# Another hand-planned order for an attention + MLP block on one core, and a later place for the last MLP's weight loads

## The chip, the core and the metric

The kernel runs on one core of a Trainium2 chip. The metric is the device time of one execution in microseconds. The core has five instruction streams that run side by side: TensorE (PE, matmuls; its weight loads are listed as PEld), VectorE (DVE), ScalarE (ACT), GpSimd (POOL), and SyncE (SP), which here issues nearly all DMAs. Each stream runs in its program order and waits on semaphores for the others.

## The reference

A transformer block with modulation, for 2048 tokens of width 640. `A_x`, all weights and `c` are bfloat16.

```python
mod = (_silu(c) @ w_mod).reshape(c.shape[0], 6, 1, -1)
sa, ca, ga, sb, cb, gb = (mod[:, 0], mod[:, 1], mod[:, 2], mod[:, 3], mod[:, 4], mod[:, 5])
h = _layernorm(x) * (1 + ca) + sa
x = x + ga * _A_ref(h, A_wqkv, A_wo)                              # 32 heads of 20, full softmax attention
h = _layernorm(x) * (1 + cb) + sb
x = x + gb * _B_ref(h, B_w_gate, B_w_up, B_w_down)                # ((h @ w_gate) * (h @ w_up)) @ w_down, width 1536
```

## The kernel before

The program is made in two steps. First a planner, written in Python in the kernel's own file, simulates the five engines with a duration for every piece of work (class `Sched`, and `pick_pe` for PE) and so fixes in which order each engine's instructions stand. Then `emit_program` writes each engine's list with the semaphore waits that the dependences need. The chip follows the order; when an instruction really starts is decided by the semaphores. The planner's numbers, such as a due time or a gate, act on the chip only through the order that results.

**The work.** The queries are cut into seven chunks (512, then six of 256). For each chunk there are eight groups of four heads; chunk times group is an *item*, 57 in all, since the last one is cut in two halves of 128 queries. Items run one after another. Within an item, the scores of a head against 128 keys at a time are computed on PE (matmul `QT`, `KT`, L1546) into PSUM banks. Most scores go to ACT, which takes two banks at a time and writes the exponentials to `PP` (L1583, 812 instructions, numbered by *progress*: progress g means that g of them have been issued in the plan). The remaining scores, in groups of four banks, are done without ACT: DVE makes an integer `DB` (L1607) and two further DVE steps and one product on POOL or DVE make the two terms `DSS` (L1639, L1647, L1659 on POOL or L1644 on DVE). Exponentials and terms are multiplied with V on PE (L2220). At the end of an item, DVE transposes the sums (`OT`, L1739), the division follows (L1747), DVE transposes back (`OcT`, L1756), and SP's copies place the rows in `Ocp` (L1768).

**What PE does beside it.** Between score matmuls PE gets three kinds of other work: probability times V (called P), projections and MLP matmuls in steps (called X: Q, K and V projections, the output projection `wo`, `Ocp`, the transposes of `h2T`, gate and up from `stg` or `stx`, down from `wd`; L982 and L978), and padding matmuls on an identity (L2553, L2581). The MLP of a chunk runs while the next chunk's attention runs; the MLP of the last chunk (`h2Tc`, `hprodc`, `xckc`) has nothing beside it and closes the kernel.

**What decides the order.** `pick_pe` is asked whenever PE is free in the plan. A score batch that is ready goes first. Otherwise named constants decide. Those that the change touches, times in nanoseconds:

- `HOLD`: PE is left idle if the next score is ready within this time.
- `FILL_MIN`: if PE's activity in the last 3413 ns of the plan is below it, X work goes ahead of P work. Before that test stands one with a fixed `FILL_HARD` of 3600, under which padding is placed.
- `PVMIN`, `PVMAX`, `PVCAP`, `PVTOL`, `PV_KEEP`: how many units of P work are needed before a batch of it starts (directly behind a score, and otherwise), the most that one takes, how far it may run past the next score, and how many free banks must remain before the next item's P work opens a bank.
- `X_LATE`, `X_HALF`: when an X step that would end after the next score is ready is split in two halves.
- `EAGER`, `D_LATE`, `D_RES`: how early DVE's scores ride along with a score batch, when they get a batch of their own, and when X work leaves banks for them.
- `XBACK`, `LKTOL`: when DVE takes the product of DVE's path from POOL, and how long POOL may hold the port that it shares with DVE when DVE has work for it.
- `STEAL_GAP`: how long ACT must be free to take an evacuation from DVE; allowed only before `STEAL_END` (66.2 us of the plan) and behind the last exponential.
- `DL`: when DVE's share of an item is due. The change leaves it as it is.

`STAGE` overrides them item by item. When the plan's P work enters an item, the constants go back to the file's defaults and the item's own entries are laid over them:

```python
    def stage(it):
        globals().update(base)
        globals().update(STAGE.get(it, {}))
```

**The last MLP's weights.** Gate and up are loaded in 12 chunks of 128 columns each, 160 KB a load. Chunks 0 to 4 go to buffers that are free once the chunk before the last no longer needs its queries; chunks 5 to 9 to buffers in the region of the projections; 10 and 11 to the ordinary staging buffers `stg`. Each load gets a gate, the progress at which the planner may first place it in SP's list:

```python
gate=int(gstart[NC] - 40) if tail and not use_x else int(gstart[NC - 1]) + 1 + STX_G * fc if tail and fc < nsq else
     NG - STX_T + int(STX_S * (fc - nsq)) if tail else ...
```

`NG` is 812 and `nsq` is 5. Among SP's ready DMAs the planner takes the one with the lowest priority number: output writes have 1, `Ocp` copies of the last two groups of heads 1.05, other `Ocp` copies 2, these weights 22. Once they stand in the list, nothing is overtaken any more: SP waits for each in its turn.

Of the kernel before, what the change touches and what calls it, by code (L numbers as in the profile page):

```python
# [35 lines left out]
STEAL_GAP = 200  # L36
HAM_W = 3413.3
HAM_MIN = 3100.0
LKTOL = 300.0
# [320 lines left out]
def emit_program(nc, sched, nsem_dma=56):  # L360
# [130 lines left out]
PV_KEEP = 2  # L491
# [10 lines left out]
EAGER = 7  # L502
# [3 lines left out]
XBACK = 0  # L506
HOLD = 110
PVTOL = 249
XDPRIO = 1.343
TPRIO = 0.75  # L510
# [20 lines left out]
D_LATE = 16  # L531
D_RES = 20
PVMIN, PVMAX, PVCAP = 2, 7, 12
# [14 lines left out]
FILL_MIN = 4190.746  # L548
# [22 lines left out]
NTERM = 2  # L571

STAGE = {
    0: {"PVMAX": 14, "XDPRIO": 1.343, "D_LATE": 16, "PVTOL": 249, "STEAL_GAP": 200, "EAGER": 4, "PVCAP": 12, "XBACK": 0, "PV_KEEP": 2, "PVMIN": 2, "HOLD": 95, "TPRIO": 0.75, "LKTOL": 300.0, "FILL_MIN": 4190.746, "X_LATE": -179.96, "D_RES": 74},
    1: {"X_HALF": 105.6, "D_RES": 62, "LKTOL": 153.5},
    2: {"DL": 0.376},
    4: {"D_RES": 31, "HOLD": 130.9, "EAGER": 12},
    5: {"D_LATE": 7, "PVMAX": 3},
    6: {"X_LATE": 168.4, "FILL_MIN": 5225.9},
    7: {"DL": 0.501, "EAGER": 12, "X_HALF": 6.3, "PVCAP": 13, "HOLD": 135.2},  # L580
    8: {"PV_KEEP": 2, "X_HALF": 103.9, "LKTOL": 307.3, "HOLD": 78.3},
    10: {"LKTOL": 95.0},
    11: {"DL": 0.443, "X_LATE": 70.4, "STEAL_GAP": 234.3},
    12: {"DL": 0.459, "PVMIN": 2, "D_LATE": 10, "LKTOL": 67.4},
    13: {"DL": 0.417, "HOLD": 108.3, "X_LATE": 6.6, "D_LATE": 17, "PVMAX": 9},
    14: {"HOLD": 73.1, "PVMIN": 2, "STEAL_GAP": 219.5},
    15: {"PVTOL": 269.4, "X_LATE": -109.7},
    18: {"HOLD": 92.2, "D_RES": 79, "PVMAX": 4, "X_HALF": 82.3},
    19: {"DL": 0.471},
    20: {"DL": 0.391, "D_RES": 12, "XBACK": 3, "FILL_MIN": 3591.0, "HOLD": 163.1},  # L590
    21: {"PVCAP": 9, "PVMAX": 2, "D_LATE": 13},
    22: {"HOLD": 191.0},
    23: {"X_HALF": -10.6, "EAGER": 3},
    24: {"DL": 0.464},
    25: {"DL": 0.549, "HOLD": 78.3, "PVMIN": 2},
    26: {"DL": 0.411, "XBACK": 3, "X_LATE": -173.2, "X_HALF": 76.9},
    27: {"DL": 0.473},
    28: {"X_LATE": -150.3, "PVMAX": 2},
    29: {"PVTOL": 317.6, "PVMAX": 4},
    30: {"D_RES": 35, "X_HALF": -38.3},  # L600
    31: {"PVMIN": 2, "FILL_MIN": 4430.1},
    32: {"PV_KEEP": 3, "PVMIN": 2},
    33: {"DL": 0.442, "FILL_MIN": 4061.0, "PV_KEEP": 2, "PVMAX": 10},
    35: {"PVMIN": 7, "LKTOL": 244.1},
    36: {"DL": 0.524, "PVMAX": 2},
    37: {"HOLD": 29.2, "PVTOL": 368.4, "PV_KEEP": 2},
    38: {"X_LATE": -201.5},
    39: {"X_LATE": 136.2},
    41: {"X_HALF": -34.1},
    43: {"XBACK": 0, "HOLD": 184.9},  # L610
    46: {"X_HALF": 35.9},
    48: {"D_LATE": 16, "FILL_MIN": 4750.6},
    50: {"FILL_MIN": 3890.7, "X_HALF": 28.4},
    51: {"X_LATE": -35.5, "XBACK": 0},
    55: {"FILL_MIN": 4927.0, "PV_KEEP": 1},
    56: {"HOLD": 80.1},
}
XHALF = 1
STG_G0, STG_G, XC_G = 12, -10, -20
X_LATE = -24.052  # L620
X_HALF = 0.0
# [2037 lines left out]
```

## Time and profile before

| what | value |
|---|---|
| median of 3 runs | 806.1 us (805.99 to 806.1) |
| the profiled execution | 807.02 us, span 805.2 us |
| PE busy | 789.9 us, 98% |
| ACT busy | 766.0 us, 95% |
| DVE busy | 701.3 us, 87% |
| POOL busy | 375.0 us, 47% |
| first exponential starts, last one starts | 16.3 us, 776.4 us |
| DMA | 64.69 MB, mean 80 GB/s |

The span is the time from the first to the last instruction of the profiled execution; the execution's own time is 1.8 us longer, and the median of the runs is 0.9 us below it. In the lists that follow, a line such as "L1583 ACT" is the instruction written by line 1583 of the kernel, on ACT; "x812" is the count. Times are in microseconds unless marked ns. Matmuls are pipelined and their ends are modelled, so 98% busy is not PE at its peak.

### The profile page before, as it was taken

The page shows a single profiled execution, that of the slowest core. Times are in us where ns is not written, and L with a number is a line of the kernel's source. Part 1 is how long each engine was busy: PE and PEld are TensorE (multiplying, and loading weights), DVE is VectorE, ACT ScalarE, POOL GpSimd, SP SyncE. Part 2 cuts the span into 40 slices and gives each one's busy share as a digit, 9 for nine tenths or more (in the row PEclk, how much of TensorE's full clock was granted, in tenths as well). Part 3 has the DMA queues.
Part 4 walks back from the last instruction along what each step waited for, and adds up shares of the span by engine and source line. Part 5 has one row for each costly group of instructions (what it writes and reads, how often), then busy time and mean ns, then how long its engine had stood idle before and what let it go on. Part 6 is the DMA issues. An engine that isn't in the chain of part 4 may idle for free.

```text
span 805.2 us, 38415 instructions
## 1 busy us (share of the span) xinstructions
PE 789.9 (98%) x16929; PEld 377.9 (47%) x16929; DVE 701.3 (87%) x1392; ACT 766.0 (95%) x853; POOL 375.0 (47%) x388
## 2 busy tenths in 40 slices
PE   8999999999999999999999999999999999999998
PEld 4443423332244443444555555555544554555567
DVE  7887988898989999998899978998789999998654
ACT  6889999999999999999999999999999999999961
POOL 3334455546445554446545464455566433344400
PEclk9999999999999999999999999999999999999999
DMA  9644222202342622110032314311530134414530
GB/s 300 204 130 116 56 56 64 62 24 73 91 108 62 188 64 61 33 40 22 23 89 67 78 54 91 69 48 48 121 73 14 48 81 103 105 33 104 127 64 18
DMA packets 154316, 64.69 MB, mean 80 GB/s; under 512 B 116951, under 2 KB 154151, under 8 KB 154151
## 3 DMA queue, kind: packets, MB, share of 16 engines
q1 hardware_dynamic: 153223, 61.10, 29.8%
q8 instruction: 134, 2.20, 1.1%
q10 hardware_dynamic: 928, 1.15, 0.5%
q14 instruction: 31, 0.25, 0.1%
HBM read 50.63 MB, written 8.99 MB: 74 GB/s over the span
## 4 chain that ended last, share of the span: by engine, by line
PE 52%; ACT 30%; DVE 12%; issue 4%; DMA 2%; SPq 1%; ACTq 0%; POOL 0%; DVEq 0%
ACT PP L1583 30%; PE ps_all L1546 18%; PE ps_all L982 15%; PE ps_all L2220 13%; PE ps_all L978 3%; DVE DB L1607 3%; PE ps_all L1249 2%; DVE hT L1154 1%; DVE st L1084 1%; DMA wm<-in_w_mod_dram 1%; DVE DSS L1644 1%; DVE DSS L1647 1%; DVE DSS L1639 1%; DMA stg<-in_B_w_up_dram 0%; SPq L1310 0%
## 5 line engine op out<-in xcount | busy, mean ns | idle before, releaser
L1583 ACT ACTIVATE PP<-ps_all 128x1024 bf16<-128x1024 f32 x812 | 748.8, 1111 | 5.2 <-PE ps_all L1546 4.5
L1659 POOL TENSOR_TENSOR DSS<-DB,DSS 128x512 bf16<-128x512 bf16 x260 | 295.8, 1158 | 302.6 <-DVE DSS L1647 247.8
L1607 DVE TENSOR_SCALAR DB<-ps_all 128x512 int16<-128x512 f32 x424 | 282.7, 681 | 49.5 <-PE ps_all L1546 47.3
L1546 PE MATMUL ps_all<-QT,KT 32*128 32x256 bf16 (+2 forms) x3648 | 320.0, 286 | 5.5 <-ACT PP L1583 3.3
L1546 PEld LDWEIGHTS ps_all<-QT,KT 32*128 32x128 bf16 x3648 | 93.2, 92 | 206.8 <-ACT PP L1583 153.8
L2220 PE MATMUL ps_all<-PP,Vf 128*32 128x256 bf16 (+2 forms) x2900 | 162.4, 290 | 0.2
L982 PE MATMUL ps_all<-h2T,stg 128*32 128x256 bf16 (+2 forms) x2720 | 124.6, 281 | 0.4 <-DVE DB L1607 0.4
L2220 PEld LDWEIGHTS ps_all<-PP,Vf 128*32 128x32 bf16 (+1 forms) x2900 | 56.3, 94 | 75.7 <-issue 69.6
L2220 PE MATMUL ps_all<-DSS,Vf 128*32 128x256 bf16 (+1 forms) x1496 | 87.4, 290 | 0.4 <-DVE DSS L1644 0.2
L1639 DVE TENSOR_SCALAR DSS<-DB 128x2048 int16<-128x2048 int16 x106 | 74.7, 705 | 0.3
L982 PEld LDWEIGHTS ps_all<-h2T,stg 128*32 128x32 bf16 x2720 | 61.5, 96 | 28.4 <-issue 22.6
L1647 DVE TENSOR_SCALAR DSS<-DB 128x2048 int16<-128x2048 int16 x106 | 72.9, 687 | 0.7 <-PE ps_all L2220 0.7
L982 PE MATMUL ps_all<-wd,hprod 128*32 128x320 bf16 (+1 forms) x1376 | 63.3, 280 | 0.4 <-DVE h2T L1922 0.2
L1644 DVE TENSOR_TENSOR DSS<-DB,DSS 128x2048 bf16<-128x2048 bf16 x41 | 51.3, 1252 | 0.0
L1747 POOL TENSOR_TENSOR OTn<-OT,invT 128x256 bf16<-128x256 f32 (+1 forms) x49 | 36.0, 735 | 32.6 <-DVE invT L1745 32.4
L2220 PEld LDWEIGHTS ps_all<-DSS,Vf 128*32 128x32 bf16 x1496 | 35.3, 95 | 21.9 <-issue 10.7
L982 PEld LDWEIGHTS ps_all<-wd,hprod 128*32 128x32 bf16 x1376 | 30.4, 96 | 18.9 <-issue 13.5
L982 PE MATMUL ps_all<-wV,hT 128*32 128x160 bf16 x1280 | 37.9, 234 | 0.9 <-DVE gab L1457 0.8
L1739 DVE STREAM_TRANSPOSE OT<-ps_all 128x256 f32<-128x256 f32 (+2 forms) x57 | 27.1, 475 | 9.2 <-PE ps_all L2220 8.7
L982 PE MATMUL ps_all<-wo,Ocp 128*32 128x320 bf16 (+1 forms) x648 | 31.1, 283 | 0.7 <-issue 0.3
L1249 PE MATMUL ps_all<-hT,wk 128*32 128x512 bf16 (+1 forms) x360 | 31.5, 382 | 0.1
L982 PEld LDWEIGHTS ps_all<-wV,hT 128*32 128x32 bf16 x1280 | 24.6, 96 | 14.7 <-issue 6.8
(133 smaller groups left out, 561.5 us busy)
## 6 DMA issues: line engine op xcount, KB each, us to landing
stg<-in_B_w_gate_dram SPq DMA_DIRECT2D x74, 160.0 KB
stg<-in_B_w_up_dram SPq DMA_DIRECT2D x74, 160.0 KB
KT<-k_rows SPq DMA_DIRECT2D x112, 32.0 KB
QT<-q_rows SPq DMA_DIRECT2D x48, 64.0 KB
Ocp<-OcT SPq DMA_DIRECT2D x164, 10.0 KB
wm<-in_w_mod_dram SPq DMA_DIRECT2D x3, 800.0 KB
x<-in_A_x_dram SPq DMA_DIRECT2D x7, 320.0 KB
k_rows<-KPA SPq DMA_DIRECT2D x16, 128.0 KB
```

Of the source, the lines that this page charges most:

```text
L982: return lambda e, b: e.matmul(ps[32 * x:32 * x + 32, b, c0 + o:c0 + o + w], lhs()[:, 32 * x:32 * x + 32], rhs() if w == n else rhs()[:, o ...
L1249: f = [lambda e, b_, k=k, x=x: e.matmul(ps[x:x + min(32, w - x), b_, :], wx[:, k, r0 + x:r0 + min(x + 32, w)], hT[tc][:, k, :], tile_posit ...
L1546: ems.append(lambda e, i=i, kt=kt: e.matmul(dstf()[:, i * u.n:(i + 1) * u.n], KT[32 * u.s:32 * u.s + 32, u.j, kt * 128:(kt + 1) * 128], QT ...
L1583: return e.activation(PPs[g % 2][:, cellp["p"], 0:nu * 512], ps[:, b0:b0 + nu, :].rearrange("p b c -> p (b c)"), AFT.Exp, scale=ESCALE)
L1607: return e.tensor_scalar(DBl[st_["slot"]][:, x * 512:(x + 1) * 512], bank(cell["b"]), EBIAS, 0.0, op0=ALU.add, op1=ALU.max)
L1639: return e.tensor_scalar(DSl[st_["ss"][0]][:, :], DBl[st_["slot"]][:, :], 0x7F, 0x3F00, op0=ALU.bitwise_and, op1=ALU.bitwise_or)
L1644: return e.tensor_tensor(d, DBl[st_["slot"]][:, :].bitcast(BF16), d, ALU.mult)
L1647: return e.tensor_scalar(DSl[st_["ss"][1]][:, :], DBl[st_["slot"]][:, :], 0x7F80, 2, op0=ALU.bitwise_and, op1=ALU.bitwise_or)
L1659: return e.tensor_tensor(d, DBl[st_["slot"]][:, x * w:x * w + w].bitcast(BF16), d, ALU.mult)
L1739: t1 = Task("dve", n * 1.1 + 84, lambda e: e.transpose(OT[:, 0:n], ps[:, item_info[it]["bank"], 0:n].rearrange("p (b q r) -> p b r q", q=3 ...
L1747: f3 = lambda e: e.tensor_tensor(OTn[:, 0:n].rearrange("p (b c r) -> p b r c", c=32, r=2), OT[:, 0:n].rearrange("p (b r c) -> p b r c", c= ...
L2220: ems.append(lambda e, i=i, kt=kt, stt=stt, stp=stp: e.matmul(ps[32 * s:32 * s + mc, bk, 0:u.n], Vf[:, (kt * H + 4 * u.j + s) * VW:(kt * H ...
```

## The change

The change touches two sets of constants and no code. `STAGE`, the table of overrides, is another one for nearly every item; only the `DL` entries stay. And the gates of weight chunks 5 to 9 of the last MLP move: with 812 exponentials, from progress 792, 793, 795, 796 and 798 to 799, 800, 801, 802 and 803. Tiling, instruction kinds, buffers, the share of scores that goes to ACT and to DVE, and the planner's durations are the same. The number of padding matmuls, of split X steps, and of products taken by DVE or POOL follows from the plan.

```diff
-STX_G, STX_T, STX_S, W_ISSUE = 3, 20, 1.5, 600.0
+STX_G, STX_T, STX_S, W_ISSUE = 3, 13, 1.0, 600.0
...
 STAGE = {
-    0: {"PVMAX": 14, "XDPRIO": 1.343, "D_LATE": 16, "PVTOL": 249, "STEAL_GAP": 200, "EAGER": 4, "PVCAP": 12, "XBACK": 0, "PV_KEEP": 2, "PVMIN": 2, "HOLD": 95, "TPRIO": 0.75, "LKTOL": 300.0, "FILL_MIN": 4190.746, "X_LATE": -179.96, "D_RES": 74},
-    1: {"X_HALF": 105.6, "D_RES": 62, "LKTOL": 153.5},
-    2: {"DL": 0.376},
-    4: {"D_RES": 31, "HOLD": 130.9, "EAGER": 12},
-    5: {"D_LATE": 7, "PVMAX": 3},
-    6: {"X_LATE": 168.4, "FILL_MIN": 5225.9},
-    7: {"DL": 0.501, "EAGER": 12, "X_HALF": 6.3, "PVCAP": 13, "HOLD": 135.2},
-    8: {"PV_KEEP": 2, "X_HALF": 103.9, "LKTOL": 307.3, "HOLD": 78.3},
...
+    0: {"D_LATE": 16, "D_RES": 74, "EAGER": 8, "FILL_MIN": 5027.9, "HOLD": 95, "PVCAP": 12, "PVMAX": 14, "PVMIN": 2, "PVTOL": 249, "X_LATE": -24.052, "PV_KEEP": 2, "STEAL_GAP": 143.6, "XBACK": 0, "LKTOL": 300.0, "X_HALF": 0.0, "TPRIO": 0.75, "XDPRIO": 1.343},
+    2: {"DL": 0.376, "PVMIN": 5},
+    3: {"PVMIN": 5},
+    6: {"X_LATE": -78.0, "FILL_MIN": 3284.6, "X_HALF": -14.5},
+    7: {"DL": 0.501},
+    8: {"PVMAX": 10, "HOLD": 164.5, "XBACK": 2},
...
-    51: {"X_LATE": -35.5, "XBACK": 0},
-    55: {"FILL_MIN": 4927.0, "PV_KEEP": 1},
-    56: {"HOLD": 80.1},
+    50: {"HOLD": 72.6},
+    52: {"HOLD": 195.5, "X_HALF": -54.0},
+    53: {"X_HALF": -14.7, "STEAL_GAP": 52.0, "D_LATE": 21, "FILL_MIN": 4907.1},
+    54: {"FILL_MIN": 4985.9, "X_LATE": 47.3, "PVTOL": 334.6},
+    55: {"PV_KEEP": 2, "FILL_MIN": 3593.0, "PVMIN": 3, "LKTOL": 200.2, "X_HALF": -100},
+    56: {"PVMIN": 6, "FILL_MIN": 5712.8, "PV_KEEP": 3},
 }
```

Item 0 lists nearly every constant because it is where the plan starts; where another item has no entry, the defaults hold (`HOLD` 110, `FILL_MIN` 4190.746, `PVMIN` 2, `PVMAX` 7, `PVCAP` 12, `PVTOL` 249, `EAGER` 7, `D_LATE` 16, `D_RES` 20, `X_LATE` -24.052, `X_HALF` 0).

More of the change, by code (lines that the diff above doesn't have):

```diff
@@ L581 @@
-    8: {"PV_KEEP": 2, "X_HALF": 103.9, "LKTOL": 307.3, "HOLD": 78.3},
[L582 to L590, printed above, removed]
@@ new lines @@
+    2: {"DL": 0.376, "PVMIN": 5},
[3 more added lines that the diff above has]
+    8: {"PVMAX": 10, "HOLD": 164.5, "XBACK": 2},
+    10: {"X_LATE": -52.4, "PVMAX": 6},
+    11: {"DL": 0.443, "PVCAP": 11, "HOLD": 119.0, "D_LATE": 9},
+    12: {"DL": 0.459},
+    13: {"DL": 0.417, "X_HALF": 108.2, "FILL_MIN": 4187.4},
+    14: {"XBACK": 0, "HOLD": 119.0, "PVCAP": 16},
+    16: {"D_LATE": 7},
+    17: {"LKTOL": 194.5, "D_LATE": 12, "X_HALF": 133.8},
@@ new lines @@
+    18: {"HOLD": 127.9, "PVMAX": 6, "X_LATE": -93.6},
+    19: {"DL": 0.471, "FILL_MIN": 3600.9},
+    20: {"DL": 0.391, "X_LATE": -112.0, "PVMIN": 3, "FILL_MIN": 3493.6},
+    21: {"PVCAP": 12, "X_LATE": 27.6},
+    22: {"EAGER": 5, "D_RES": 12},
+    23: {"X_HALF": -42.8, "HOLD": 93.3, "EAGER": 8, "STEAL_GAP": 263.1, "PVMAX": 7},
+    24: {"DL": 0.464},
+    25: {"DL": 0.549, "PV_KEEP": 1, "X_HALF": 36.5, "PVTOL": 177.7, "X_LATE": -69.3},
+    26: {"DL": 0.411, "EAGER": 7, "FILL_MIN": 5119.4, "X_LATE": -10.9},
@@ new lines @@
+    27: {"DL": 0.473, "PVTOL": 151.8, "PV_KEEP": 1, "PVCAP": 15},
+    29: {"X_HALF": 53.6, "D_RES": 14},
+    30: {"PVTOL": 368.9, "X_HALF": -24.6},
+    31: {"D_RES": 74, "PVMIN": 3, "FILL_MIN": 5015.2},
+    32: {"X_LATE": 76.2},
+    33: {"DL": 0.442, "PVMIN": 2, "EAGER": 8},
+    35: {"HOLD": 76.0, "PVMAX": 8},
+    36: {"DL": 0.524, "X_LATE": -52.4, "PVMAX": 7, "X_HALF": -72.9, "D_RES": 80},
+    37: {"LKTOL": 352.0, "PVTOL": 312.4},
+    39: {"X_LATE": 0.7, "HOLD": 131.2, "STEAL_GAP": 161.3},
@@ new lines @@
+    41: {"PV_KEEP": 3, "X_HALF": -94.5},
+    43: {"X_HALF": 62.7},
+    44: {"X_LATE": 47.4},
+    45: {"X_HALF": 14.7},
+    47: {"X_HALF": -31.0, "HOLD": 115.1},
+    50: {"HOLD": 72.6},
[4 more added lines that the diff above has]
+    56: {"PVMIN": 6, "FILL_MIN": 5712.8, "PV_KEEP": 3},
```

22 lines of the change are left out of this document (removed).

## The prediction

> **What bounds the kernel now.** I read the page first, then the exponentials stretch by stretch, the waits, and the tail instruction by instruction.
>
> ```profile
> PE 789.9 (98%) x16929; PEld 377.9 (47%) x16929; DVE 701.3 (87%) x1392; ACT 766.0 (95%) x853; POOL 375.0 (47%) x388
> PEclk9999999999999999999999999999999999999999
> PE 52%; ACT 30%; DVE 12%; issue 4%; DMA 2%; SPq 1%; ACTq 0%; POOL 0%; DVEq 0%
> L1583 ACT ACTIVATE PP<-ps_all 128x1024 bf16<-128x1024 f32 x812 | 748.8, 1111 | 5.2 <-PE ps_all L1546 4.5
> L2553 PE MATMUL ps_all<-ident,Vf x136: 272/273/389, 62.4 to 709.9; 128*32 128x256 bf16 x112, 128*32 128x512 bf16 x24
> ```
>
> ACT's 812 exponentials and PE's matmuls are both close to full, and the chain that ended last goes back and forth between them. Neither alone is the bound: a plan gains only where it keeps PE from delivering a score late, or leaves PE less to do behind the last exponential. The change alters no exponential, projection or MLP matmul; it alters their order, and the few that the planner adds as padding (L2553).
>
> The windows of the exponentials alone (busy us, count) separate three parts.
>
> ```profile
> 0.00:60.00 60.00, 35.09 (x38) 1.00 0.68 212
> 60.00:740.00 680.00, 676.99 (x736) 1.00 0.28 70
> 740.00:778.00 38.00, 36.73 (x40) 1.00 0.48 103
> 439.72 21.19 ACT L1583 ACTIVATE PP<-ps_all 128x1024 bf16<-128x1024 f32 x23
> ACT PP L1583 <- PE ps_all L1546: 2.6, 8, 0.5
> 654.24 7.62 ACT L1583 ACTIVATE PP<-ps_all 128x1024 bf16<-128x1024 f32 x8
> 662.30 5.61 ACT L1583 ACTIVATE PP<-ps_all 128x1024 bf16<-128x1024 f32 x6 [0.43 <-PE ps_all L1546]
> ```
>
> The row at 439.72 is an unbroken run: neighbours overlap, so with the mean of one exponential (1.111 us, L1583 above) the pitch is (21.19 - 1.11)/22 = 0.913 us. The middle has 736 of them, 736 x 0.913 = 672 us, in 680. So the middle loses 8 us to late scores, of which 680 - 677.0 = 3.0 us is visible idle time; the remainder is exponentials that come a little late one by one. Eight idle waits there are named (2.6 us). What one costs is read from start to start: 654.24 to 662.30 is 8.06 us for eight exponentials worth 8 x 0.913 = 7.30, so 0.76 us. I use 0.76 us as the price of a late score.
>
> The tail, behind the last exponentials:
>
> ```profile
> 749.58 27.84 ACT L1583 ACTIVATE PP<-ps_all 128x1024 bf16<-128x1024 f32 x30 [0.52 <-PE ps_all L1546]
> 779.06 0.32 PE L982 MATMUL ps_all<-wd,hprodt 128*32 128x320 bf16 x4
> 779.83 0.59 PE L982 MATMUL ps_all<-wd,hprodt 128*32 128x320 bf16 x12
> 780.73 1.27 PE L982 MATMUL ps_all<-wd,hprodt 128*32 128x320 bf16 x32
> 782.14 2.91 PE ps_all L978 x49
> 785.33 17.23 PE ps_all L978 x251
> 760.00:776.00 16.00, 15.74 (x416) 9.56 (x417) 3.82 (x12) 15.96 (x18) 0.62 (x1) 1.00 0.64 135
> ```
>
> The last exponential ends at 749.58 + 27.84 = 777.42. Then PE finishes the down projection of the sixth MLP (wd, hprodt), 0.32 + 0.59 + 1.27 = 2.18 us, and from 782.14 runs the last MLP without a break until 785.33 + 17.23 = 802.56. That stretch is fixed work.
>
> **The change, part by part.** The profiled execution took 807.02 us with a span of 805.2; the median is 806.1. I add the terms to 807.02 and take them over to the median unchanged.
>
> (1) *Head, item 0.* Its row changes STEAL_GAP from 200 to 143.6 (ACT takes evacuations from DVE sooner), EAGER 4 to 8, X_LATE -180 to -24, FILL_MIN 4191 to 5028.
>
> ```profile
> 16.33 7.54 ACT L1583 ACTIVATE PP<-ps_all 128x1024 bf16<-128x1024 f32 x8
> 23.84 0.59 ACT L1259 CAST KPA<-ps_all 128x512 bf16<-128x512 f32 x1
> 26.13 7.61 ACT L1583 ACTIVATE PP<-ps_all 128x1024 bf16<-128x1024 f32 x8 [0.24 <-PE ps_all L1546]
> 36.95 7.44 ACT L1583 ACTIVATE PP<-ps_all 128x1024 bf16<-128x1024 f32 x8 [0.55 <-PE ps_all L1546]
> 47.40 13.86 ACT L1583 ACTIVATE PP<-ps_all 128x1024 bf16<-128x1024 f32 x15 [0.58 <-PE ps_all L1546]
> ```
>
> Three breaks, where the next 512 keys are not ready: 16.33 to 47.40 is 31.07 us for 24 exponentials worth 21.9, a loss of 9.2 us. In each break ACT has time to spare, so one more stolen cast (0.59) is hidden, or at worst pushes each restart by 0.59: +1.8. If it frees DVE for the keys by as much, -1.8. I take 0, since the breaks (about 3 us each) are far longer than a cast. All later STEAL_GAP entries do nothing: stealing is allowed only before 66 us and behind the last exponential.
>
> (2) *Middle, 60 to 740 us.* Here nearly all the new entries act. Bounds: -8 (every late score gone) and, by the rows nearest to it, +6.1 (eight more late scores at 0.76). An order picked because it still holds when durations and landings shift should lose some of the waits that arise because something landed later than planned. I take two of the eight named waits away, 2 x 0.76 = -1.5. That is nearer to no change than to either end, because most of the 8 us is small lateness that no row assigns to a place.
>
> (3) *The last items' priorities.* In items 53, 54 and 56 FILL_MIN goes up to 4907, 4986 and 5713 (all three had 4191), in 55 it goes down from 4927 to 3593. A higher value makes PE take MLP and projection work before probability-times-V. The transposes that close items 53, 54, 55 and 56 place them:
>
> ```profile
> 752.73 0.45 DVE L1739 STREAM_TRANSPOSE OT<-ps_all 128x256 f32<-128x256 f32 x1
> 763.52 0.45 DVE L1739 STREAM_TRANSPOSE OT<-ps_all 128x256 f32<-128x256 f32 x1 [3.50 <-PE ps_all L2220]
> 771.49 0.32 DVE L1739 STREAM_TRANSPOSE OT<-ps_all 128x128 f32<-128x128 f32 x1 [2.92 <-PE ps_all L2220]
> 778.27 0.30 DVE L1739 STREAM_TRANSPOSE OT<-ps_all 128x128 f32<-128x128 f32 x1
> ```
>
> Item 54 thus lies at about 753 to 763 and 56 at 771 to 778. The most that can go is the 2.18 us left behind the exponentials; the same amount can be added. But PE has only 16 - 15.74 = 0.26 us idle from 760 to 776, so what is done earlier pushes probability-times-V later. I take -0.4: the idle time, and a little from fewer switches of kind of work.
>
> (4) *Weights of the last MLP.* Ten loads (chunks 5 to 9, gate and up) are asked for from progress 799 to 803 instead of 792 to 798. What counts is their place among SP's other issues:
>
> ```profile
> 758.27 0.48 SPq L1959 DMA_DIRECT2D stx<-in_B_w_gate_dram  x1
> 764.94 0.31 DVE L1756 STREAM_TRANSPOSE OcT<-OTn 128x128 f32<-128x128 f32 x1
> 764.96 0.66 SPq L1959 DMA_DIRECT2D stx<-in_B_w_up_dram  x1
> 765.66 1.75 SPq L1959 DMA_DIRECT2D stg<-in_B_w_up_dram  x1
> 767.46 4.38 SPq L1768 DMA_DIRECT2D Ocp<-OcT  x5
> 771.88 11.77 SPq L2099 DMA_DIRECT2D out_dram<-xckt  x2
> 773.32 0.72 PE L978 MATMUL ps_all<-wo,Ocp 128*128 128x320 bf16 x4
> 744.95 3.77 DMA stg<-in_B_w_up_dram
> ```
>
> Progress 799 is the 17th of the run of 30: 749.58 + 16 x 0.913 = 764.2 us, and 803 comes at 767.8. Item 54's five Ocp copies are ready at 765.25 and waited 2.2 us behind the loads; they now go after the first pair or so. The remaining loads follow them and, at about 1.1 us a pair (five pairs and two stg loads took 758.27 to 767.41), are out by about 775. A load lands 3.77 us after its issue (row of 744.95), so by 779. PE wants chunk 5 in the third round of the last MLP: 20 matmuls take about 1.2 us (49 in 2.91), so 782.14 + 2.4 = 784.5. The loads stay hidden with 5 us to spare. The copies' 2.2 us bring the output projection forward, but the PE work above covers that chain. Term: 0; bounds -0.3 and +4.0 (rival 3).
>
> Sum: 0 - 1.5 - 0.4 + 0 = -1.9; 807.02 becomes 805.1, and the median 806.1 becomes 804.2.
>
> *The granted clock.* It is full in all 40 slices, and the emptiest 5 us after 700 us still had it; only when PE has run dry at the end does it fall:
>
> ```profile
> 745.00:750.00 5.00, 4.35 (x118) 2.29 (x114) 3.98 (x10) 4.48 (x6) 3.16 (x3) 1.00 0.67 142
> 804.00:805.20 1.20, 0.00 (x0) 0.00 (x0) 0.00 (x0) 0.00 (x0) 0.00 (x0) 0.83 0.20 70
> ```
>
> Items 6 and 55 now have FILL_MIN at 3285 and 3593 (5226 and 4927 before), below the fixed 3600 under which padding matmuls are forced. So padding may come where useful work came (a padding matmul takes 0.27 us, L2553), and the planner watches PE's recent activity less closely there. Since a stretch with PE 87% busy kept the full clock, I give this no term. [...]
>
> **The rivals.** (1) *Waits exchanged, no net change:* the new order cures some late scores and makes others; 806.1, from 804.5 to 807.7. For it: ACT and PE are 95 and 98% busy, and the eight named waits are a mere 2.6 us. Against: the entries of nearly every item differ, so cancellation has to be lucky.
>
> (2) *More late scores in the middle, slower:* a plan that hedges has a longer nominal path, and larger batches of probability-times-V (PVMIN 5 in items 2 and 3, 6 in 56; PVMAX 10 in 8) hold PE when a score is due. Place: wherever PE starts such a batch just before a bank comes free. Price 0.76 each; three more and it shows, four give 806.1 + 3.0 = 809.1, eight 812.2. For it: 98% busy PE leaves nothing to recover with. Against: 8 us of lateness is spread thinly already.
>
> (3) *Weights late:* if one pair stands behind SP's second output write, whose issue ended at 771.88 + 11.77 = 783.65, it lands at about 783.65 + 1.1 + 3.77 = 788.5, 4.0 past the need: 810.1. It decides only if the plan places that write ahead of the pair; 768 and 783 are far apart, so 4%.
>
> (4) *The clock falls while work runs:* a lull in item 6 or 55 lets the clock go as it does behind the last matmul; 10 us at the 0.83 of that row become 12.0, so +2.0 and 808.1. 3%: nothing in the middle comes near an idle PE. [...]
>
> **How the numbers follow.** A measurement can tell about 0.2% (1.6 us) from no change. Forecast 804.2 and that side: 0.40; no net change 0.27; more late scores 0.26; weights 0.04; clock 0.03. Slower together: 0.33. The low end takes six of the eight named waits away: 806.1 - 6 x 0.76 - 0.4 = 801.1; the high end is the weights' case, 810.1, which also holds five more late scores (809.9). The forecast's own range is 801.9 (five waits go) to 804.4 (where a change begins to show). Cases of both signs hold most of the chance; the direction is the weak part.
>
> **What would show it.** Right: eight named waits of exponentials on scores in the middle become about six, the last exponential ends near 775.9, less than 2.18 us of wd, hprodt matmuls come behind it, item 54's Ocp issues begin near 765.3, and the last MLP still runs unbroken. Wrong: the last exponential ends later than 779, with more idle time in front of exponentials; or PE waits for stx in the last MLP; or a clock below 1.00 in the middle.

## The result, and the profile after

The changed kernel takes 804.61 us (median of 14 runs, 804.12 to 807.59), the kernel before 806.2 us on the same chip (14 runs, 805.84 to 807.27). The ratio is 0.998, with a 95% interval of 0.9971 to 0.9988: faster by 0.2%, or 1.6 us. The prediction was 804.2. The profiled execution took 804.69 us with a span of 802.9, so 2.33 us less than before's 807.02; that execution of before lies 0.8 us above its median, so the pair of traces shows more than the medians do.

The page after, lines that answer to those shown of before:

```profile
PE 789.0 (98%) x17069; PEld 381.1 (47%) x17069; DVE 702.6 (88%) x1395; ACT 766.1 (95%) x852; POOL 366.2 (46%) x380
PE 67%; DVE 15%; ACT 13%; issue 3%; DMA 1%; SPq 1%; POOL 0%; ACTq 0%; DVEq 0%
L1583 ACT ACTIVATE PP<-ps_all 128x1024 bf16<-128x1024 f32 x812 | 748.8, 1110 | 4.8 <-PE ps_all L1546 3.8
```

PE and ACT are as busy as they were, within 0.9 us; DVE does 1.3 us more and POOL 8.8 us less (366.2 against 375.0). The idle time in front of the exponentials fell by only 0.4 us (5.2 to 4.8). The chain that ended last shifts from ACT (30% to 13%) to PE (52% to 67%), which by itself does not say where time was won.

The windows of the exponentials on ACT (busy us, count, granted clock, DMA share, GB/s), and the named waits from 60 to 740 us:

```profile
0.00:60.00 60.00, 36.01 (x39) 1.00 0.70 216
60.00:740.00 680.00, 677.34 (x736) 1.00 0.29 70
740.00:778.00 38.00, 35.45 (x39) 1.00 0.45 94
ACT PP L1583 <- PE ps_all L1546: 2.0, 7, 0.4
ACT PP L1583 <- PE ps_all L2220: 0.2, 1, 0.2
```

From 60 to 740 us there are 736 exponentials, as before, and eight named waits, as before (2.2 us in all instead of 2.6). The last window is shorter of work because one more exponential was done before 60 us. By windows alone one would say that the gain is the head's. The starts of single exponentials say otherwise. First the timeline of ACT, after:

```profile
46.37 12.96 ACT L1583 ACTIVATE PP<-ps_all 128x1024 bf16<-128x1024 f32 x14 [0.54 <-PE ps_all L1546]
...
150.78 49.60 ACT L1583 ACTIVATE PP<-ps_all 128x1024 bf16<-128x1024 f32 x54 [0.22 <-PE ps_all L1546]
...
639.77 14.78 ACT L1583 ACTIVATE PP<-ps_all 128x1024 bf16<-128x1024 f32 x16
654.85 119.58 ACT L1583 ACTIVATE PP<-ps_all 128x1024 bf16<-128x1024 f32 x130 [0.29 <-PE ps_all L1546]
774.59 1.02 ACT L1583 ACTIVATE PP<-ps_all 128x1024 bf16<-128x1024 f32 x1 [0.16 <-PE ps_all L1546]
```

and the rows of the same view of before that the prediction did not need:

```profile
88.78 111.96 ACT L1583 ACTIVATE PP<-ps_all 128x1024 bf16<-128x1024 f32 x122 [0.32 <-PE ps_all L1546]
...
639.76 22.11 ACT L1583 ACTIVATE PP<-ps_all 128x1024 bf16<-128x1024 f32 x24
...
668.16 63.84 ACT L1583 ACTIVATE PP<-ps_all 128x1024 bf16<-128x1024 f32 x69 [0.26 <-PE ps_all L1546]
732.19 16.88 ACT L1583 ACTIVATE PP<-ps_all 128x1024 bf16<-128x1024 f32 x18 [0.19 <-PE ps_all L1546]
```

Counting back from the last exponential, the same one starts at 47.40 before and at 46.37 after: the head wins 1.03 us. Both views that begin in the head end at 200 us, and the last exponential that they hold is the same one, the 190th. It ends at 88.78 + 111.96 = 200.74 before and at 150.78 + 49.60 = 200.38 after: 0.36 is left. The exponential with 147 to go starts at 639.76 and at 639.77: nothing is left. Between these two places the distance wanders, from 0.75 us earlier to 0.5 later, without a trend. Behind 640 us, before has four restarts (662.30, 668.16, 732.19, 749.58); after has one at 654.85, then 130 exponentials without a named break, and one short wait for the last. The last exponential ends at 774.59 + 1.02 = 775.61, against 777.42: 1.81 us, all of it won in the last 136 us, about 1.0 of it by 740 us.

One pair of executions could mislead, so here are the others. `w_only`, `load_early` and `load9_early` (below) keep the order of before on PE, ACT, DVE and POOL; in their traces the exponential with 147 to go starts at 639.77 to 640.13. In `o_only`, which keeps the order of after, it starts at 639.60. From there to the end of the last exponential the four executions of the old order take 137.3 to 137.7 us, the two of the new order 135.7 and 135.8.

The tail (start, length, engine, line, tiles, count; then three steps of the chain that ended last, and one of before's):

```profile
768.95 0.32 DVE L1739 STREAM_TRANSPOSE OT<-ps_all 128x128 f32<-128x128 f32 x1 [2.31 <-PE ps_all L2220]
776.35 0.73 PE L982 MATMUL ps_all<-wd,hprodt 128*32 128x320 bf16 x16
778.09 1.27 PE L982 MATMUL ps_all<-wd,hprodt 128*32 128x320 bf16 x32
780.46 0.44 PE L978 MATMUL ps_all<-wo,OcT 128*128 128x320 bf16 x2
...
778.09 1.36 DVE h2Tc L1901 x5
779.50 5.25 PE ps_all L978 x88
785.09 15.16 PE ps_all L978 x214
...
780.79 1.30 DVE h2Tc L1901 x5
```

The last MLP starts at 779.50 instead of 782.14, which is 2.64 us earlier, and PE ends at 785.09 + 15.16 = 800.25 instead of 802.56: 2.31. Of the 2.64, 1.81 are the exponentials; the other 0.83 is a shorter way from the last exponential to the last MLP (3.89 us instead of 4.72). Part of the 0.83 is given back: two output-projection matmuls of the second half (`wo`, `OcT`), which stood ahead of the last MLP before, now stand in it at 780.46 (88 + 214 matmuls against 49 + 251), so that it takes 20.75 us instead of 20.42. The way from the last exponential to PE's end is thus 0.50 us shorter.

Behind the last exponential there are still 48 down-projection matmuls, as before. What came earlier is item 55's closing transpose, at 768.95 instead of 771.49 (of these 2.54 us, 1.81 come with the exponentials), then the output projection and the layer norm of the first half of the last chunk. In both traces the chain that ended last runs through that layer norm: its last step on DVE, `h2Tc`, ends at 778.09 + 1.36 = 779.45 after and at 780.79 + 1.30 = 782.09 before, and the last MLP starts 0.05 us behind it.

### The profile page after: what moved, and what is told of

Read it like the earlier page. It is cut to its first block, busy times and chain, and to the rows that moved or that the text cites. A ratio compares the mean times of both kernels' runs of the same rounds, so it can differ in the third digit from the quotient of the medians.

```text
span 802.9 us, 38700 instructions
## 1 busy us (share of the span) xinstructions
PE 789.0 (98%) x17069; PEld 381.1 (47%) x17069; DVE 702.6 (88%) x1395; ACT 766.1 (95%) x852; POOL 366.2 (46%) x380
## 3 DMA queue, kind: packets, MB, share of 16 engines
q8 instruction: 135, 2.21, 1.2%
## 4 chain that ended last, share of the span: by engine, by line
PE 67%; DVE 15%; ACT 13%; issue 3%; DMA 1%; SPq 1%; POOL 0%; ACTq 0%; DVEq 0%
PE ps_all L1546 23%; PE ps_all L982 20%; PE ps_all L2220 16%; ACT PP L1583 13%; DVE DB L1607 4%; PE ps_all L1249 4%; PE ps_all L978 3%; DVE DSS L1647 2%; DVE DSS L1639 1%; DVE hT L1154 1%; DVE h2T L1922 1%; DMA wm<-in_w_mod_dram 1%; DVE DSS L1644 1%; PE ps_all L1185 1%; DVE OT L1739 1%
## 5 line engine op out<-in xcount | busy, mean ns | idle before, releaser
L1659 POOL TENSOR_TENSOR DSS<-DB,DSS 128x512 bf16<-128x512 bf16 x252 | 286.4, 1156 | 301.9 <-DVE DSS L1647 246.5
L1607 DVE TENSOR_SCALAR DB<-ps_all 128x512 int16<-128x512 f32 x424 | 281.4, 681 | 47.2 <-PE ps_all L1546 45.4
L2220 PEld LDWEIGHTS ps_all<-PP,Vf 128*32 128x32 bf16 (+1 forms) x2900 | 54.1, 94 | 77.0 <-issue 69.8
L982 PEld LDWEIGHTS ps_all<-h2T,stg 128*32 128x32 bf16 x2832 | 64.1, 96 | 28.9 <-issue 22.0
L1647 DVE TENSOR_SCALAR DSS<-DB 128x2048 int16<-128x2048 int16 x106 | 76.1, 718 | 0.3 <-PE ps_all L2220 0.3
L1639 DVE TENSOR_SCALAR DSS<-DB 128x2048 int16<-128x2048 int16 x106 | 73.2, 691 | 0.5
L982 PE MATMUL ps_all<-wd,hprod 128*32 128x320 bf16 (+1 forms) x1356 | 61.2, 281 | 0.1
L1747 POOL TENSOR_TENSOR OTn<-OT,invT 128x256 bf16<-128x256 f32 (+1 forms) x49 | 36.5, 745 | 42.0 <-DVE invT L1745 42.0
L1644 DVE TENSOR_TENSOR DSS<-DB,DSS 128x2048 bf16<-128x2048 bf16 x43 | 53.5, 1245 | 0.1
L1249 PE MATMUL ps_all<-hT,wq 128*32 128x512 bf16 x375 | 31.8, 382 | 0.0
```

Source lines behind the costliest of these rows:

```text
L982: return lambda e, b: e.matmul(ps[32 * x:32 * x + 32, b, c0 + o:c0 + o + w], lhs()[:, 32 * x:32 * x + 32], rhs() if w == n else rhs()[:, o ...
L1249: f = [lambda e, b_, k=k, x=x: e.matmul(ps[x:x + min(32, w - x), b_, :], wx[:, k, r0 + x:r0 + min(x + 32, w)], hT[tc][:, k, :], tile_posit ...
L1607: return e.tensor_scalar(DBl[st_["slot"]][:, x * 512:(x + 1) * 512], bank(cell["b"]), EBIAS, 0.0, op0=ALU.add, op1=ALU.max)
L1639: return e.tensor_scalar(DSl[st_["ss"][0]][:, :], DBl[st_["slot"]][:, :], 0x7F, 0x3F00, op0=ALU.bitwise_and, op1=ALU.bitwise_or)
L1644: return e.tensor_tensor(d, DBl[st_["slot"]][:, :].bitcast(BF16), d, ALU.mult)
L1647: return e.tensor_scalar(DSl[st_["ss"][1]][:, :], DBl[st_["slot"]][:, :], 0x7F80, 2, op0=ALU.bitwise_and, op1=ALU.bitwise_or)
```

## The experiments

Each kernel was timed against the kernel before in the same series. That kernel's median was 806.53 to 806.73 us in these series and 806.2 in the first one, so medians of different series can be compared to about 0.5 us; the ratios are within a series. The edits are shown in short; those to the table only say which rows were taken. Added lines shift the line numbers of these kernels by up to 23; the exponentials are always the group `PP<-ps_all` on ACT.

### Which of the two edits

```diff
# w_only: before, with the new gates; only SP's list differs from before
-STX_G, STX_T, STX_S, W_ISSUE = 3, 20, 1.5, 600.0
+STX_G, STX_T, STX_S, W_ISSUE = 3, 13, 1.0, 600.0
# o_only: after, with the old gates; only SP's list differs from after
-STX_G, STX_T, STX_S, W_ISSUE = 3, 13, 1.0, 600.0
+STX_G, STX_T, STX_S, W_ISSUE = 3, 20, 1.5, 600.0
```

> The kernel before, with only the gates of the last MLP's weight chunks 5 to 9 moved (STX_T 13, STX_S 1.0). Only SP's list differs; PE, ACT, DVE and POOL have the order of before. Theory A (the order alone makes the gain, the weights are worth nothing): 806.2 +- 0.3, the same as before. Theory B (the weights' later place frees item 54's Ocp copies and shortens the tail): 805.0 to 805.7, with the first wo,Ocp matmul of the last chunk earlier than 773.3.

> The changed kernel with the old gates of weight chunks 5 to 9 (STX_T 20, STX_S 1.5); only SP's list differs from the changed kernel. Theory A: 804.6 +- 0.3, the whole gain. Theory B: 805.1 to 805.8.

The gates alone: 806.63 us against 806.67, ratio 0.9995 (0.9984 to 1.0006). The order alone: 804.61 us, 0.9972 (0.9961 to 0.9984), the same as the whole change. So the order is the whole gain. With the gates alone, the timeline of SP and PE shows

```profile
765.60 2.98 SPq L1768 DMA_DIRECT2D Ocp<-OcT  x4
773.64 0.72 PE L978 MATMUL ps_all<-wo,Ocp 128*128 128x320 bf16 x4
```

Four of the five `Ocp` copies did move ahead, to 765.60 from 767.46, as the prediction worked out. The output projection that reads them began at 773.64, where it began at 773.32 before: PE's order places it there, and it did not wait for the copies.

### Which part of the order

```diff
# early45: new rows for items 0 to 45, old rows for 46 to 56, new gates
# late46:  old rows for items 0 to 45, new rows for 46 to 56, old gates
+STAGE = {k: (NEW if k <= 45 else OLD)[k] for k in ...}     # early45; late46 the other way round
```

> The new rows of STAGE for items 0 to 45, the old rows for items 46 to 56, the new gates. Until P work enters item 46 the order is that of the changed kernel. The traces of before and after part company for good near there (exponential 660 is 0.4 us later after the change, the last one 1.8 us earlier). Theory C (each row carries its gain where it acts; the late rows made it): 806.2 to 806.6, the gain is lost and no more. Theory D (a row fits only the state that the rows ahead of it leave): slower than both kernels, 807 to 810.

> The mirror image: old rows for items 0 to 45, new rows from 46 on, old gates. Until P work enters item 46 the order is that of the kernel before. Theory C: about 804.4, the whole gain of the late rows. Theory D: slower than both, 807 to 811, since the new late rows meet a state that they were not chosen for.

Neither half has the gain: 807.62 us, ratio 1.0009 (0.9996 to 1.0022), and 808.62 us, 1.0022 (1.0013 to 1.003). The second is slower than before. By the ratios the two together give -1.6 us; one by one they give +0.7, which is not clear of noise, and +1.8 (1.0009 and 1.0022 of 806.67). So the effects of rows do not add. That a row's numbers fit the state in which the rows ahead leave the plan (theory D of the expectations) agrees with this; no run tests it further. The traces show how each half loses. The new late rows on the old start (start, length, engine, tiles, count):

```profile
760.24 16.08 ACT L1584 ACTIVATE PP<-ps_all 128x1024 bf16<-128x1024 f32 x17 [0.17 <-PE ps_all L1547]
...
778.98 0.59 PE L983 MATMUL ps_all<-wd,hprodt 128*32 128x320 bf16 x12
780.52 3.58 PE L983 MATMUL ps_all<-wd,hprodt 128*32 128x320 bf16 x100
784.03 1.51 PE L979 MATMUL ps_all<-h2Tc,stx 128*128 128x128 bf16 x24
```

The last exponential ends at 776.32, 1.1 us earlier than before; yet 112 down-projection matmuls are left behind it instead of 48, and the last MLP starts at 784.03. The new early rows with the old end:

```profile
773.84 2.86 ACT L1582 ACTIVATE PP<-ps_all 128x1024 bf16<-128x1024 f32 x3 [0.30 <-PE ps_all L1545]
781.18 0.45 PE L1888 MATMUL ps_all<-ident,xn2c 128*128 128x128 bf16 x5 [0.55 <-DVE xn2c L1872]
783.23 1.74 PE L977 MATMUL ps_all<-h2Tc,stx 128*128 128x128 bf16 x28 [0.41 <-DVE h2Tc L1900]
```

Here too the last exponential is early (776.70), and PE then waits for DVE's layer norm. So the last exponential is not what sets the time. What does is when the last MLP starts: in all 14 profiled executions of this study, 20.4 to 20.75 us pass from there to PE's end. And for that start three things must be done together: the exponentials, the sixth chunk's MLP, and the layer norm of the first half.

### Is the new order steadier

The prediction took the new order for one picked because it holds when durations and landings shift. If that is how it wins (theory S), then with durations and landings disturbed on purpose it must lose less than the old one; if it wins by a shorter path (theory N), it need not.

```diff
# dist_before, dist_after: the same additions on both kernels
+if t.name is one of 35 score steps of DVE: e.tensor_reduce(jsb[:, k:k+1], junk, ...)   # DVE held 0.67 us
+if i >= 150 and i % 8 == 3 and i < 680: e.dma_start(JD[...], JX[0:128, :])              # SP: 66 copies of 160 KB
```

> The kernel before with disturbances that its plan does not know: on DVE a reduction of 512 elements into a spare column in front of one score conversion in every third quad (35 of them, about 0.5 us each), and on SP a 160 KB copy from HBM to HBM behind every eighth place of its list from the 150th on (67 of them), each costing SP an issue and the DMA queues their time. Order and arithmetic are otherwise those of before; the extra results are not used. Theory S (the new order gains because it has slack): this one loses clearly more than the changed kernel under the same disturbance; the distance grows from 2.0 us to 3.5 or more. Theory N (the gain is not slack but a shorter path): both lose alike, the distance stays 2.0 +- 0.8. Both theories: 810 to 825.

> The changed kernel with the same disturbances at the same quads and at the same places of SP's list. Theory S: 3.5 us or more below the disturbed kernel before. Theory N: 1.2 to 2.8 us below it.

820.17 us, ratio 1.0161 (1.0138 to 1.0184), for the old order; 821.38 us, 1.0173 (1.0147 to 1.0198), for the new. The disturbance costs the old order 13.6 us and the new one, from its own 804.6 of another series, about 16.8. Neither theory's distance came out: the new order was forecast 1.2 us or more below the old one and is 1.2 above it, within the noise. The groups show that it did bite:

```profile
L454 DVE TENSOR_REDUCE jsb<-ident 128x1 f32<-128x512 bf16 x35 | 23.4, 669 | 0.0
jit_rows<-in_A_x_dram SPq DMA_DIRECT2D x66, 160.0 KB, 2.7
ACT PP L1606 <- PE ps_all L1569: 15.9, 36, 1.5
```

That last line is the named waits of the whole execution of the new order; undisturbed it has 12 of them, 3.8 us. In the old order they go from 12 (4.5 us) to 28 (12.1 us). So the new order is not steadier against this disturbance, and its lead is gone: the intervals overlap. Part of the cost is the clock, which fell in both:

```profile
220.00:225.00 5.00, 3.21 (x58) 1.05 (x56) 2.57 (x4) 3.33 (x5) 2.74 (x3) 0.98 0.45 128
225.00:230.00 5.00, 5.00 (x68) 1.43 (x64) 2.73 (x6) 3.49 (x4) 0.00 (x0) 0.68 0.26 77
```

(windows of the disturbed old order: busy us and count of PE, PEld, DVE, ACT, POOL, then the granted clock). It fell once in the profiled execution of the old order (mean 0.998) and twice in that of the new (mean 0.996; 0.50 from 682.40 to 685.60), so one pair of executions does not rank them. Another kind of disturbance was not tried.

### What a late score costs in the end

The prediction priced a late score at 0.76 us and let it count fully at the end. If the order had room to win back time (theory P), it would not. One exponential was held up by a small copy from HBM.

```diff
# delay_e40: in the changed kernel, on ACT; delay_e700 the same before exponential 700
+if t.name == "E40":
+    e.dma_start(sched.dly[0], sched.dly[1][0:128, 0:64]).then_inc(dsem, 16)
+    e.wait_ge(dsem, 16)
```

> The changed kernel with ACT held up once, in front of exponential 40 (at about 61 us): it issues a small copy from HBM to HBM and waits for it to land, some 2 to 3 us. Theory P (lost exponential time early on is won back, since PE goes on with other work and later has less of it; this is how the 1.3 us that the change gained in the head went by 200 us): at the end less than half of the hold is left, +0 to +1.0 us. Theory E (each exponential is a bound from here to the end): the whole hold, +2 to +3 us.

> The same hold in front of exponential 700 (at about 672 us). Theory P: PE's leftover work shortens by part of it, +1 to +2 us, more than at exponential 40 because less time is left. Theory E: the whole hold, as at exponential 40.

The holds came out at 1.08 and 1.79 us, shorter than the 2 to 3 that were expected. The medians are 806.81 us (1.0008, 0.999 to 1.0026) and 807.62 us (1.0018, 1.0001 to 1.0036), 2.2 and 3.0 us above 804.6. In 9 of 12 runs of each the mean granted clock was 0.991 to 0.998, so the medians hold more than the lateness. The three runs of each with the full clock took 805.52 to 805.85 and 806.18 to 806.38 us, 0.9 to 1.2 and 1.6 to 1.8 above 804.6: near the two holds. The profiled executions say what became of one hold:

```profile
674.07 102.05 ACT L1589 ACTIVATE PP<-ps_all 128x1024 bf16<-128x1024 f32 x111 [1.79 <-DMA dly_rows<-in_A_x_dram]
776.28 1.02 ACT L1589 ACTIVATE PP<-ps_all 128x1024 bf16<-128x1024 f32 x1 [0.16 <-PE ps_all L1552]
```

That is the hold at exponential 700: 1.79 us of idle time. Exponential 700 starts 1.80 us later than in the trace of after, and the last one at 776.28 instead of 774.59, 1.69 later. 111 exponentials later, nothing has been won back to speak of; PE's end is 1.70 later. The hold at exponential 40, 1.08 us:

```profile
62.52 3.77 ACT L1589 ACTIVATE PP<-ps_all 128x1024 bf16<-128x1024 f32 x4 [1.08 <-DMA dly_rows<-in_A_x_dram]
65.00:70.00 5.00, 5.00 (x58) 1.35 (x57) 3.36 (x7) 4.20 (x5) 2.93 (x3) 0.66 0.29 74
776.37 1.02 ACT L1589 ACTIVATE PP<-ps_all 128x1024 bf16<-128x1024 f32 x1 [0.16 <-PE ps_all L1552]
```

The clock fell for 3.4 us behind it (0.66 over that window), so that exponential 60 was 2.4 us late; about that stood until exponential 680, half a microsecond came back near there, and the last one is 1.78 late. Lateness is carried nearly whole, over 770 exponentials (theory E). This is why the head's lead of 1.03 us must have been lost somewhere in particular, and was: the trace of after has small waits at 94.92, 131.21 and 150.78 us, where before runs on from 88.78 to beyond 200.

### One late load of before

Before's wait at 749.58 stands behind a late weight pair, whose second load takes 3.77 us to land (shown in the prediction). Is it what the new order avoids?

```diff
# load_early: before, one pair of loads on stg, near 750 us, ahead of three Ocp copies in SP's list
# load9_early: the same for chunk 9's pair
+move(sc.all["SP"], pair, ahead_of=three_Ocp_copies)
```

> The kernel before with one move in SP's list: the pair of loads of the sixth MLP's last weight chunk (gate and up) goes ahead of three of the five Ocp copies behind which it stood at 744.1 us. All other lists are those of before. In the trace of before PE waited for this pair (3.77 us from issue to use, PE idle 0.65 us, the exponentials 0.70 us late at 748 us). Theory W (this one wait is part of what the new order cures between exponentials 760 and 790): the pair lands about 2.1 us earlier, the exponentials from 784 on run 0.5 to 0.7 us earlier, and the end with them: 805.5 to 805.9. Theory Q (what counts is PE's total work, and such a wait is made good in the tail): 806.3 +- 0.3 as before.

> The kernel before with the pair of loads that its trace shows late (chunk 9 of the sixth MLP, issued at 744.1 and 744.95 us) moved ahead of three of the five Ocp copies in front of it; all other lists are those of before. The move tried earlier took chunk 11's pair, which stands at 750 us and was not late. Theory W: the pair goes out at about 741.5, some 2.4 us earlier, PE's idle 0.65 us on it disappears, the exponentials from 784 on run 0.5 to 0.7 us earlier, and the span is 0.5 to 0.7 us shorter, since a hold on the exponentials at 672 us came out at the end in full. Theory Q: the tail makes it good either way; span and time as before, within 0.3 us.

The first moved chunk 11's pair, which was not the late one, so that it says nothing on the question: 806.57 us, 0.9998 (0.9989 to 1.0007), with a wait of 0.68 us still at 749.32. The second moved the right pair: 806.4 us, 0.9997 (0.9988 to 1.0006).

```profile
732.84 44.59 ACT L1583 ACTIVATE PP<-ps_all 128x1024 bf16<-128x1024 f32 x48 [0.46 <-PE ps_all L1546]
745.00:750.00 5.00, 5.00 (x137) 2.77 (x132) 4.44 (x10) 5.00 (x7) 3.82 (x4) 1.00 0.36 81
```

The wait is gone, the exponentials run through from 732.84, and PE is busy all of 745 to 750 (4.35 of 5 before). The last exponential still ends at 777.43, since this execution was 0.4 to 0.5 us late from the head on; relative to exponential 740 the last one gains 0.37 us. The median does not move. So this load explains at most some 0.4 us of before's late stretch, and that too is not shown at the end of the kernel.

### A shorter plan without regard to slack

If a shorter undisturbed path is what counts (theory N), an order chosen for that alone should do at least as well.

```diff
# plan_short: after's rows, those from item 6 on altered by a random search for an earlier planned finish and nothing else
-    6: {"X_LATE": -78.0, "FILL_MIN": 3284.6, "X_HALF": -14.5},
+    6: {"X_LATE": -78.0, "FILL_MIN": 4044.0, "X_HALF": -14.5},
...
-    53: {"X_HALF": -14.7, "STEAL_GAP": 52.0, "D_LATE": 21, "FILL_MIN": 4907.1},
+    53: {"X_HALF": -14.7, "STEAL_GAP": 52.0, "D_LATE": 21, "D_RES": 30, "X_LATE": -31.7, "FILL_MIN": 4240.7},
```

> A third order: the changed kernel's STAGE, its rows from item 6 on altered by a random search for nothing but an earlier finish in the planner's own undisturbed count; no disturbance and no margin in the search. Weights' gates as in the changed kernel. Theory N (an earlier planned finish carries over to the chip, hedged or not): 803.0 to 804.2, below the changed kernel. Theory S (the changed kernel is fast because its order was chosen for slack, and a search without disturbances gives that up): 804.6 to 806.5.

803.73 us (five runs, 803.52 to 804.17), ratio 0.9964 (0.9951 to 0.9978): the lowest median of this study. The changed kernel was not timed in this series; its median in the first was 0.9 us higher, its interval there (0.9971 to 0.9988) overlaps this one a little, and that of `o_only` (0.9961 to 0.9984) does more. So the third order beats the one of before, and is at least as good as the changed one.

```profile
639.41 135.13 ACT L1588 ACTIVATE PP<-ps_all 128x1024 bf16<-128x1024 f32 x147
778.62 4.30 PE ps_all L983 x71
783.20 16.11 PE ps_all L983 x231
```

Its last 147 exponentials run in one piece of 135.13 us, (135.13 - 1.11)/146 = 0.918 us from start to start, close to the 0.913 of an unbroken run; before took 777.42 - 639.76 = 137.66 for them, and after 775.61 - 639.77 = 135.84. With no late score left there, the last MLP starts at 778.62. The search asked for no slack, and the time did not suffer. That does not exclude theory S by itself, since the search started from the changed kernel's rows and kept many of them; what the disturbed kernels showed stands beside it.

### The padding and the clock

```diff
# nopad_after: the changed kernel without the padding matmuls on zeros (L2553)
-for i, f in enumerate(t.emits):
+for i, f in enumerate(() if t.name == "zfill" else t.emits):
```

> The changed kernel without the padding matmuls on the running sums (the zero terms; those of the head stay). They add zero, so the result is that of the changed kernel. Theory K (the padding holds the clock and costs next to nothing where PE had no other work): the clock stays 1.00 or dips; 804.4 to 806. Theory L (padding delays scores): fewer late scores, 803.8 to 804.3.

807.8 us (11 runs, 805.68 to 813.04), ratio 1.0015 (0.9999 to 1.0032), 3.2 us above the changed kernel's median of the first series. All 11 runs had a mean granted clock below full, 0.989 to 0.998; of the changed kernel's 14 runs, 13 had 1.000 and one 0.998, and that one took 807.59 us. The kernel before had a mean clock below full in 5 of its 87 runs in the series of these experiments (809.53 to 812.29 us). The windows of the first place where it fell:

```profile
65.00:70.00 5.00, 4.36 (x55) 1.71 (x55) 4.98 (x10) 5.00 (x7) 3.77 (x4) 0.75 0.28 68
70.00:75.00 5.00, 5.00 (x54) 1.38 (x55) 4.28 (x7) 3.69 (x5) 1.05 (x2) 0.57 0.21 51
```

In the profiled execution the clock stood at half for 6.8 us from 67.5 and again from 705.8 (0.50 over 67.60 to 74.20 and over 705.90 to 712.50), and each time cost 1.7 to 1.9 us. So the padding earns its place, also when the 0.5 us between the series is allowed for. The changed kernel has 184 padding matmuls, 10.6 us of PE, where before had 136 and 7.5 us.

## Why the prediction was right, and where it was not

The sum came out (804.2 predicted, 804.6 measured; 2.33 us in the profiled execution where 1.9 was predicted) and so did the side, which the prediction had given a chance of 0.40. Its terms did not come out as reasoned, so that the sum fits is in good part luck.

**Term (1), the head: 0.** Right as a sum, by another way than it gave. The head did win 1.03 us (46.37 against 47.40), inside the bounds of 1.8, and lost it again: 0.36 us of it stood at 200 us, none at 640.

**Term (2), the middle: -1.5.** The step that failed is "two of the eight named waits": eight stay. A gain of about that size came in the late stretch, 1.81 us behind 640 us, of which the term's window of 60 to 740 held about 1.0. The reason given for it (an order that holds under shifted durations loses fewer waits) has no support: disturbed, the new order was no better, and an order searched further for an earlier finish alone was at least as fast. The price of 0.76 us for one late score was not measured again. That lateness counts fully at the end, on which the term rested, is shown: of the hold at exponential 700, 1.80 us at its start are 1.69 at the last one.

**Term (3), the last items: -0.4.** About right in size, by another way. From the last exponential to PE's end 0.50 us were won. The term looked for them in the 2.18 us of down projection left behind the last exponential. These stayed, 48 matmuls in 0.73 + 1.27 = 2.00 us. What shortened the way to the last MLP by 0.83 us was the layer norm of the first half, ready earlier because item 55 closed at 768.95 and not 771.49; 0.33 went back into the last MLP. The prediction took that for fixed work without a break. It is not fixed: 20.42 us became 20.75. Nor is it without a break: five transposes of the second half stand in it, for 0.34 us at 784.75 after and for 0.28 us before (the prediction's own lines, 782.14 + 2.91 = 785.05, then 785.33). The prediction had quoted the row of item 55's transpose but not followed what waits for it. The two halves of the order on the chip show that this way can cost more than it gained here: 784.03 and 783.23 for the start of the last MLP, though their exponentials ended early.

**Term (4), the weights: 0.** Right, and shown alone (0.9995, 0.9984 to 1.0006). Four copies went out at 765.60 in that kernel as worked out, and PE did not need them earlier. The reason given, that PE's work covers the chain of the output projection, is too strong: in both kernels the chain that ended last runs through it. It is PE's order, not the copies, that says when it starts. In the changed kernel SP's list was

```profile
756.34 0.48 SPq L1959 DMA_DIRECT2D stx<-in_B_w_gate_dram  x1
763.40 4.31 SPq L1768 DMA_DIRECT2D Ocp<-OcT  x5
772.25 0.52 SPq L1959 DMA_DIRECT2D stx<-in_B_w_up_dram  x1
779.93 0.36 SPq L2099 DMA_DIRECT2D out_dram<-xckt  x1
```

with the last weight load issued at 772.25 and the second output write at 779.93, behind it, so that rival 3 did not happen. The copies began at 763.40, not near 765.3, because item 54 itself closed earlier (its `OcT` ends at 763.37 instead of 765.25).

**The signals.** The last exponential was forecast to end at 775.9 and ended at 775.61. The last MLP runs as unbroken as it did before, with two more matmuls in it. It was forecast that the eight waits become six; they stayed eight. Less than 2.18 us of down projection was forecast, which is true only by 0.18.

**The rivals.** Rival 1 (exchange, no net change) is what happened up to 640 us. Rival 2 (late scores, slower) is what the late half of the order does by itself: 808.62 us, near the 809.1 given for four more late scores, though through work left behind the last exponential and not through late scores. Rival 4 (the clock falls) was given 3%, because nothing in the trace came near an idle PE. That argument was wrong: without the padding the clock fell in all 11 runs (means of 0.989 to 0.998), in one stretch where PE is 87% busy by the profile (4.36 of 5 us, clock 0.75), at 1.7 to 1.9 us a time. That this is near the 2.0 worked out is chance: the 0.83 of the row at 804.00 is the mean of a stretch in which the clock fell at 804.80 (1.00 up to there, 0.50 from 804.85 to 805.20), and the two falls without padding held 0.50 for 6.8 us each. In the changed kernel it hardly fell (0.998 in one run of 14, 1.000 in the others); that padding as a whole keeps it up is shown by these two sets of runs, that the 48 added matmuls do is not.

**What stays open.** Which single decisions of the order make the late stretch whole. The halves show that effects of rows do not add, and no run here separates them. How far a different sort of disturbance would favour one of the orders is also open.

## What to carry to other kernels

When a hand-planned order leaves two engines both about full, follow one numbered instruction through both traces, counted from the end: windows and named waits put the gain in the wrong place here, and the starts of the same exponential put it behind 640 us at once. Delay was carried to the end nearly one for one here (1.80 us at exponential 700, 1.69 at the last one), so look for a shorter planned path, which was enough here, and test the whole order on the chip, since good rows of a table need not combine. And find the one start that fixes the end (here the last MLP's), and list everything that must be ready for it, not only the engine that was busiest.

## What the runs showed of the hardware that was not expected

The granted clock fell with PE idle for only 0.67 to 1.79 us just before it. Windows of 5 us hide most of what goes before: in the delayed kernel PE was 4.01 of 5 us busy from 60 to 65 us, and the clock was at half from 65.11 to 68.53 (worked out from 0.78 over 65.00 to 65.20, 0.62 over 68.30 to 68.60 and 0.66 over 65 to 70); without padding 4.36 of 5 went with a fall; yet before had 4.35 of 5 from 745 to 750 with the full clock, 1.00. Stretches of 3.41 us, as long as that fall, say more (columns as above; the delayed kernel and the one without padding, each up to the start of a fall, then a stretch of the disturbed new order that no fall followed):

```profile
61.70:65.11 3.41, 2.42 (x46) 1.29 (x46) 2.80 (x6) 2.59 (x3) 0.56 (x1) 1.00 0.35 101
64.08:67.49 3.41, 2.74 (x45) 1.14 (x41) 3.39 (x7) 3.41 (x5) 2.95 (x3) 1.00 0.34 99
224.88:228.29 3.41, 2.11 (x36) 0.72 (x39) 1.98 (x3) 2.35 (x4) 2.39 (x3) 1.00 0.30 90
```

Ahead of the six falls in the traces of this study PE was busy for 1.62 to 2.74 of 3.41 us, so it was without work for 0.67 to 1.79 us each time. But the stretch at 224.88, with 2.11, kept the full clock, and so did 671.15 to 674.56 in the kernel held at exponential 700, with 2.21. The busy time of PE therefore does not decide it by itself. What the clock does answer to was not measured.

A fall cost less than half of its length. One of 3.4 us cost about 1.2 us in the head (2.4 us of lateness, of which the hold made 1.2) and 1.3 in the disturbed new order (682.3 to 685.7: against the trace of after, exponential 693 starts 16.44 us late and exponential 695 17.75), where half is 1.7. The two of 6.8 us without padding cost 1.7 to 1.9, where half is 3.4.

DVE and POOL slowed each other in places. In the trace of before, DVE's steps L1639 and L1647 took 0.68 us on average, and never over 0.70, with no POOL instruction beside them; beside POOL's L1747 at 306.56 (1.07 us, where its mean is 0.68) one L1639 took 0.80 and one L1647 1.10. DVE's L1607 took 0.68 on average with POOL busy beside it and without. What the two engines share was not measured.
